# Spreading the sums of weights over two blocks, and a seventh weight buffer in block 4

## The chip, the core and the metric

The kernel runs on one core of a Trainium2 chip. The metric is the device time of one execution in microseconds (us), the median of several runs. The engines are TensorE (PE in the profile), VectorE (DVE), ScalarE (ACT), GpSimd (POOL) and SyncE (SP), which here does nothing but issue transfers.

## What is computed

Three stages follow one another, on 3072 tokens of width 512, all in float32.

```
for t in range(768):                       # 4 batches x 8 heads x 64
    state = gamma * state + k_t v_t^T
    y_t   = scale * q_t state              # decaying attention
x  = y                                     # 3072 tokens x 512
xn = x / sqrt(mean(x*x) + 1e-6) * rms_g
x  = (silu(xn @ w_gate) * (xn @ w_val)) @ w_out          # d_ff 1536
h  = x @ w_in                                            # d_ff 1024
s  = h * softmax(h)
out = ((s - mean s) / sqrt(var s + 1e-6) * g_ln) @ w_out2
```

## The kernel before

The tokens are worked in six blocks of 512, numbered 0 to 5. Attention of the next block runs inside the matmuls of the block in hand, as do the norm of the next block and the second feed-forward layer of the last one. A float32 operand is split into a high and a low half (tiles ending in h and l: `xnh`, `xnl`), and each product is three matmuls, hi x hi, lo x hi and hi x lo (L844 to L846).

In blocks 0 to 3 (`bc_block`) the inner width 1536 is cut into twelve pieces m of 128. Each m has three phases on TensorE: gate (bank GB, followed by the silu on ScalarE, L896), value (bank VB, followed by the product on VectorE, L865, whose result is split at L101 and L102), and out (bank X, with the tiles `wo`). Each phase ends at a slot, so a block has 36 slots of the first layer, a few us each, and some more for the second. Side work is hung on the slots as lists of Python functions (`extra`); tables at the head of the file say which slot. The order on each engine comes from a scheduler that keeps these lists roughly in order.

Blocks 4 and 5 (`shared_block` and `seven_block`, L960) use a seven-product scheme for pairs of m: instead of eight products of quarter blocks there are seven, of sums of quarters. For this the kernel prepares sums of the weights in blocks 1 to 3: `sums_steps(j, part, n)` adds two weight tiles on POOL (L622), then takes four quarter sums (L641), splits the results on VectorE and ScalarE (`parts`), and stores them to DRAM (`sscr`, L656 and L658). Two tiles take part, X (the sums) and H (the split results of its first half). `SUMS` and `LATE_SUMS` give the block and the slot. `w2_sums(k)` does the same for the second layer's weights (L674, L680, stored to `t2scr`), and `W2_SUMS_AT` gives its slots in block 2.

Four resources order this work. The tag `x2` has four rotating tiles of 512 KB, which the sums use in blocks 1 to 3; a new tile waits until the store of the tile's last user has landed. POOL is one queue in order: behind the sums stand the decay of the attention state (L282), which VectorE's update of the state (L279) waits for, and behind that update, on VectorE, the row sums of the norm (L350) and the product L865. SP is one queue too: a transfer that waits for a tile holds up all that stand behind it. DMA semaphores are eight, taken in turn.

In block 4 the weights and their sums come as half tiles, fourteen to a pair j of m, two to a 512 KB buffer (`fit`); six buffers rotate, four of tag `w4` and two of tag `x2`. L1056 and L1058 load a buffer in one transfer, L1061 in two. The first two `wo` tiles of block 4 are issued from slot 56 of block 3 (L773), ahead of the seventh buffer load, and their tiles are free once POOL has split the last tiles of x (L102).

Of the kernel before, what the change touches and what calls it, by code (L numbers as in the profile page):

```python
# [36 lines left out]
SUMS = {1: [(3, 0), (3, 1)], 2: [(0, 0), (0, 1), (1, 0), (1, 1), (4, 0)], 3: [(2, 0), (2, 1), (4, 1)]}  # L37
LATE_SUMS = {(3, 1): (5, 0), (3, 5): (5, 1)}
W2_SUMS_AT = (13, 20)
# [4 lines left out]
def retention_moe_kernel(ctx: ExitStack, tc: tile.TileContext, qk0, q2, kt, kv, wpk, w2i, w2o,  # L44
# [564 lines left out]
    def sums_steps(j, part, n):  # L609

        X, H = [], []
        small = n == 1 and part == 0

        def pair(t):
            if small:
                t.extend(wt("A" if t is X else "r2", [P, 512], F32, 2 if t is X else 8) for _ in range(2))
            else:
                x = wt("x2", [P, 2, 512], F32, 4)
                t.extend((x[:, 0, :], x[:, 1, :], x))

# [31 lines left out]
        def store():  # L652
            for t, at in ((H, 0), (X, 2)):
                if small:
                    for i in range(2):
                        nc.sync.dma_start(sscr[j][part][:, at + i], t[i].rearrange("p (s x) -> p s x", s=2))  # L656
                else:
                    nc.sync.dma_start(sscr[j][part][:, at:at + 2], t[2].rearrange("p a (s x) -> p a s x", s=2))  # L658

        if (j, part) in SUMS.get(n, ()):  # L660
            at0, at1 = 6 * j + part, 6 * j + 3 + part
            return {at0: [lambda: whole(0)], at1: [lambda: whole(1), sums], at1 + 2: [parts], at1 + 3: [store]}
        return {0: [load], 2: [both, sums], 4: [parts], 5: [store]}
# [3 lines left out]
    def w2_sums(k):  # L667
# [18 lines left out]
        def parts():  # L686
            for t in (W[0][:, 0, :], W[1][:, 1, :]):
                o.append(wt("x2", [P, 2, 512], F32R, 4))
                tied(o[-1][:, 0, :], o[-1][:, 1, :], t)

        def parts2():
            tied(w2["h"][:, k, 512:], w2["l"][:, k, 512:], W[1][:, 0, :])
            h, l = (wt("st", [P, 512], F32R, 3) for _ in range(2))
            tied(h, l, W[0][:, 1, :])
            o.extend((h, l))

        def store():
            for i in range(2):
                nc.sync.dma_start(t2scr[i][:, :, k, :], o[i].bitcast(F32))

        def store2():
            for i in range(2):
                nc.sync.dma_start(t2scr[2][:, i, k, :], o[2 + i].bitcast(F32))
# [338 lines left out]
    def fit_load(tiles):  # L1042

        def source(j, part, q):
            if q in (0, 4, 6):
                return scr[2 * j + (q == 6)][part][:, :, lo if q == 0 else hi]
            return sscr[j][part][:, (0, 2, 3, None, 1)[q - 1]]

        for T in tiles:
            t = fit[T % len(fit)]  # L1050
            tf = t.bitcast(F32)
            keys = [((2 * T + i) // 14, (2 * T + i) // 7 % 2, (2 * T + i) % 7) for i in range(2)]
            stock.update((key, t[:, i]) for i, key in enumerate(keys))
            (j, part, q), S = keys[0], sscr[keys[0][0]][keys[0][1]]
            if q == 2:
                nc.sync.dma_start(tf, S[:, 2:4])  # L1056
            elif q == 1:
                nc.sync.dma_start(tf.rearrange("p a s x -> p a (s x)"), S[:, 0:3:2].rearrange("p a s x -> p a (s x)"))  # L1058
            else:
                for i, key in enumerate(keys):  # L1060
                    nc.sync.dma_start(tf[:, i], source(*key))  # L1061

    NT = 7 * NM // 2

    def fit_first(n):
        fit.extend(wt("w4", [P, 2, 2, 256], F32R, 4) for _ in range(4))
        fit_load(range(2))
# [4 lines left out]
    def fit_last(n):  # L1072
        fit.extend(wt("x2", [P, 2, 2, 256], F32R, 4) for _ in range(2))
        fit_load(range(4, 6))

    def shared_block(n):
# [3 lines left out]
        pairs = [(wt("r2", [P, 512], F32R, 8), wt("r2", [P, 512], F32R, 8)) for _ in range(3)]  # L1080
# [30 lines left out]
        def last_outs():  # L1111
            t, w = fit[2].rearrange("p a b x -> p a (b x)"), tuple(wt("A", [P, 512], F32R, 2) for _ in range(2))
            nc.sync.dma_start(t.bitcast(F32), scr[NM - 2][2])
            for k in range(2):
                nc.sync.dma_start(w[k].bitcast(F32), scr[NM - 1][2][:, k, :])
            wsp[base + NM - 2, 2], wsp[base + NM - 1, 2] = t, w

        for j in range(NM // 2):
            m = 2 * j
            final = m == NM - 2  # L1120
            g = phase1(j, 0)
            slot(n, 6 * j)
# [18 lines left out]
            if final:  # L1141
                out(m - 2, range(3, NK))
# [7 lines left out]
            for i in range(2):  # L1150
                if i:
                    V.tensor_tensor(out=vf[:, 512:], in0=vf[:, 512:], in1=gf[:, 512:], op=ALU.mult)
                ah, al = pairs[nact[0] % 3]
# [4 lines left out]
            if final:  # L1158
                out(m - 1)
# [421 lines left out]
    for n in range(NB):  # L1581
        if n + 1 < NB:
# [15 lines left out]
            if n + 1 in SEVEN:  # L1598
                r = (30, 32) + ((33, 34, 34, 34, 34) if n + 1 < NB - 1 else (35,) * 5) + (36, 50, 50, 50)
                r += (39, 40, 41, 42) if n + 1 == NB - 1 else (54, 54, 54, 55)  # L1600
                begun7, more7 = (lambda: seven_load(n + 1), seven_pump) if n + 1 == NB - 1 else \
                    (lambda: fit_first(n + 1), lambda: fit_more(n + 1))
                first7 = [begun7] + [lambda i=i: w_load((n + 1) * NM + i, 2) for i in range(2)] + [more7]
                if n + 1 < NB - 1:
                    extra.setdefault((n, 54), []).append(lambda: fit_last(n + 1))
                for s, f in zip((47, 48, 48, 51) if n + 1 == NB - 1 else (47, 56, 56, 51), first7):
# [95 lines left out]
```

## Time and profile before

| | |
|---|---|
| median of three runs | 982.71 us (981.64 to 983.69) |
| profiled execution | 981.34 us, of which its span is 979.5 us |
| PE busy | 955.9 us, 98% of the span |
| DVE, ACT, POOL busy | 557.7, 418.0, 462.0 us |
| bytes moved | 230.91 MB, 236 GB/s in the mean |

TensorE is busy nearly throughout. What is left over is some 24 us of idle time in the span, at a few places, and the time that matmuls take longer where the granted clock is low. The page's mean rates hide how uneven the transfers are: in some stretches of block 4 the DMA engines are busy without a break, while just before they have little to do.

### The profile page before, as it was taken

Reading aid. Unit: us, or ns where it says so; the run is one execution under the profiler, and the core shown is the slowest. Engines: PE = TensorE matmul, PEld = TensorE weight load, DVE = VectorE, ACT = ScalarE, POOL = GpSimd, SP = SyncE. Lnnn points to the kernel's source line nnn. Section 1 sums busy time; section 2 is a strip of 40 time slices with the busy share of each in tenths; the row PEclk is TensorE's granted clock in tenths of the full one; section 3 lists DMA queues with packets and bytes.
Section 4 is the critical chain, followed back from the end, with each engine's and each line's share of the span. In section 5 each row is a group of like instructions: output and inputs, shape, how many; then the busy total and the mean of one; then the engine's idle time right before and its main releaser. Section 6 shows DMA issues by size and latency. Waiting matters only on the chain.

```text
span 979.5 us, 18179 instructions
## 1 busy us (share of the span) xinstructions
PE 955.9 (98%) x6852; PEld 805.3 (82%) x6852; DVE 557.7 (57%) x1126; ACT 418.0 (43%) x831; POOL 462.0 (47%) x497
## 2 busy tenths in 40 slices
PE   8999999999999999989999999999899999999998
PEld 7878787887887888778888888888788988999987
DVE  4788766565375644465574442574555467343473
ACT  3757656475344343223454231346212256321254
POOL 6876853696053394784538344546111166000022
PEclk9799999999999999999999999999999999999999
DMA  9699999897823306989824889823999936688501
GB/s 342 232 321 398 362 321 349 300 342 252 296 61 97 94 22 228 295 303 295 320 98 148 295 267 297 285 95 96 284 287 350 302 127 220 215 302 293 192 1 44
DMA packets 98887, 230.91 MB, mean 236 GB/s; under 512 B 11632, under 2 KB 38640, under 8 KB 97776
## 3 DMA queue, kind: packets, MB, share of 16 engines
q1 hardware_dynamic: 90016, 204.59, 62.6%
q10 hardware_dynamic: 8784, 25.17, 6.7%
q8 instruction: 54, 0.88, 0.4%
q14 instruction: 33, 0.27, 0.1%
HBM read 187.77 MB, written 41.94 MB: 235 GB/s over the span
## 4 chain that ended last, share of the span: by engine, by line
PE 77%; DMA 8%; DVE 5%; POOL 3%; ACT 3%; issue 1%; SPq 0%; ACTq 0%; POOLq 0%; DVEq 0%
PE X L844 9%; PE X L846 9%; PE X L845 9%; PE GB L844 5%; PE GB L845 5%; PE GB L846 5%; PE VB L960 4%; PE VB L844 4%; PE VB L845 4%; PE VB L846 4%; PE GB L960 3%; PE X L1359 3%; PE SB L122 3%; PE GB L1359 2%; PE VB L1359 2%; PE YB L960 2%
## 5 line engine op out<-in xcount | busy, mean ns | idle before, releaser
L845 PE MATMUL X<-r,wo 128*128 128x512 f32 x252 | 99.0, 393 | 0.0
L745 POOL TENSOR_TENSOR st<-st,x 128x512 int32<-128x512 int32 x52 | 70.3, 1353 | 59.6 <-ACT x L742 21.4
L846 PE MATMUL X<-r,wo 128*128 128x512 f32 x252 | 98.3, 391 | 0.0
L844 PE MATMUL X<-r,wo 128*128 128x512 f32 x252 | 96.4, 399 | 1.0 <-ACT r L101 1.0
L865 DVE TENSOR_TENSOR f<-VB,f 128x512 f32<-128x512 f32 x48 | 33.1, 689 | 69.2 <-PE VB L846 56.8
L101 ACT CAST r<-f 128x512 fp32r<-128x512 f32 x60 | 37.1, 620 | 80.5 <-DVE f L865 60.7
L844 PE MATMUL VB<-xnh,w 128*128 128x512 f32 (+1 forms) x172 | 68.0, 395 | 3.1 <-DVE f L865 3.1
L102 DVE TENSOR_TENSOR r<-f,r 128x512 fp32r<-128x512 f32 x60 | 58.1, 969 | 19.3 <-ACT r L101 18.6
L844 PE MATMUL GB<-xnh,w 128*128 128x512 f32 (+1 forms) x172 | 67.7, 393 | 0.9 <-ACT f L896 0.5
L845 PE MATMUL GB<-xnl,w 128*128 128x512 f32 (+1 forms) x172 | 67.1, 390 | 0.5 <-DVE xnl L102 0.4
L846 PE MATMUL VB<-xnh,w 128*128 128x512 f32 (+1 forms) x172 | 67.1, 390 | 0.3 <-POOL w L102 0.3
L845 PE MATMUL VB<-xnl,w 128*128 128x512 f32 (+1 forms) x172 | 67.1, 390 | 0.0
L846 PE MATMUL GB<-xnh,w 128*128 128x512 f32 (+1 forms) x172 | 66.7, 388 | 0.0
L282 POOL TENSOR_TENSOR U<-U,u 128x256 f32<-128x256 f32 x27 | 17.7, 654 | 96.6 <-PE YB L122 59.2
L102 POOL TENSOR_TENSOR r<-st,r 128x512 fp32r<-128x512 f32 x4 | 5.2, 1300 | 116.3 <-ACT r L101 116.3
L896 ACT ACTIVATE f<-GB 128x512 f32<-128x512 f32 x48 | 28.5, 594 | 69.8 <-PE GB L846 69.6
L844 PE MATMUL X<-w2oh,r 128*128 128x512 f32 (+1 forms) x144 | 56.6, 393 | 0.5 <-ACT r L1222 0.5
L844 PEld LDWEIGHTS X<-r,wo 128*128 128x128 f32 x252 | 47.5, 190 | 10.8 <-ACT r L101 1.1
L846 PE MATMUL X<-w2oh,r 128*128 128x512 f32 (+1 forms) x144 | 56.1, 390 | 0.2 <-DVE r L1223 0.2
L846 PEld LDWEIGHTS X<-r,wo 128*128 128x128 f32 x252 | 47.5, 188 | 10.0
L845 PE MATMUL X<-w2ol,r 128*128 128x512 f32 (+1 forms) x144 | 55.5, 385 | 0.0
L845 PEld LDWEIGHTS X<-r,wo 128*128 128x128 f32 x252 | 47.6, 189 | 9.5 <-issue 0.2
(511 smaller groups left out, 2751.0 us busy)
## 6 DMA issues: line engine op xcount, KB each, us to landing
w<-scr SPq DMA_DIRECT2D x73, 512.0 KB, 6.0
wo<-scr SPq DMA_DIRECT2D x57, 512.0 KB, 5.5
x<-in_wpk SPq DMA_DIRECT2D x36, 512.0 KB, 6.6
sscr<-x SPq DMA_DIRECT2D x22, 512.0 KB, 6.0
rv<-in_kv SPq DMA_DIRECT2D x40, 256.0 KB, 6.5
scr<-CV ACTq DMA_DIRECT2D x18, 512.0 KB, 6.7
w<-scr SPq DMA_DIRECT2D x34, 256.0 KB, 5.8
w<-sscr SPq DMA_DIRECT2D x14, 512.0 KB, 5.9
```

What stands on the lines that cost most here:

```text
L101: h = nc.scalar.copy(hi, src)
L102: (lo_eng or nc.vector).tensor_tensor(out=lo, in0=src, in1=hi.bitcast(F32), op=ALU.subtract)
L122: return lambda: nc.tensor.matmul(out, lhsT=lhsT, rhs=rhs, start=start, stop=stop)
L282: nc.gpsimd.tensor_tensor(out=new, in0=old, in1=u64.unsqueeze(2).to_broadcast([P, 4, 64]), op=ALU.mult)
L745: nc.gpsimd.tensor_tensor(out=ti, in0=ti, in1=lo, op=ALU.add)
L844: nc.tensor.matmul(ps, lhsT=lh, rhs=rh, start=start, stop=False)
L845: nc.tensor.matmul(ps, lhsT=lh, rhs=rl, start=False, stop=False)
L846: return nc.tensor.matmul(ps, lhsT=ll, rhs=rh, start=False, stop=stop)
L865: recent["dve"] = nc.vector.tensor_tensor(out=a, in0=GV[1], in1=silu[:, 0, :], op=ALU.mult)
L896: recent["act"] = nc.scalar.activation(s[:, 0, :], GV[0], AF.Silu)
L960: recent["seven"] = nc.tensor.matmul(ps, lhsT=x, rhs=y[:, k, :], start=start and k + i == 0, stop=k == 1 and i == 2, skip_group_check=True)
L1359: last["mm"] = nc.tensor.matmul(bank, lhsT=x[:, k, ts_], rhs=y[:, k, :], start=start and k + i == 0, stop=k == 1 and i == 2, skip_group_ch ...
```

## The change

Five sums stay where they were or change their block: in block 2 the sums of (0,0), (1,0) and (4,0) remain, and (0,1) and (1,1) move to block 3. Splits come one or two slots later than before, stores two slots after the split. The late sum (5,0) is loaded one slot later, (5,1) nineteen slots later. The second layer's sums start one slot and two slots earlier (12 and 18 for 13 and 20); their splits no longer take `x2` tiles of their own but are written in place, and their stores are cut accordingly. In block 3 the H tiles of (0,1) and (1,1) are pairs of tag `r2`.

In block 4 a seventh weight buffer is made of two tiles of tag `r2`; for that the pairs that hold the split product go from three to two. The first two `wo` tiles are issued behind the loads of the buffers. Two of the four steps that sum quarters of x move from slot 54 to 53 of block 3. The last out(m - 1) of block 4 is called earlier.

```diff
-SUMS = {1: [(3, 0), (3, 1)], 2: [(0, 0), (0, 1), (1, 0), (1, 1), (4, 0)], 3: [(2, 0), (2, 1), (4, 1)]}
-LATE_SUMS = {(3, 1): (5, 0), (3, 5): (5, 1)}
-W2_SUMS_AT = (13, 20)
+SUMS = {1: [(3, 0), (3, 1)], 2: [(0, 0), (1, 0), (4, 0)], 3: [(0, 1), (1, 1), (2, 0), (2, 1), (4, 1)]}
+LATE_SUMS = {(3, 2): (5, 0), (3, 24): (5, 1)}
+W2_SUMS_AT = (12, 18)
...
-        small = n == 1 and part == 0
+        tags = {(1, 0): ("A", "r2"), (3, 1): ("x2", "r2")}.get((n, part) if n == 1 or j < 2 else None, ("x2", "x2"))
...
-            return {at0: [lambda: whole(0)], at1: [lambda: whole(1), sums], at1 + 2: [parts], at1 + 3: [store]}
-        return {0: [load], 2: [both, sums], 4: [parts], 5: [store]}
+            wait = 2 if j == 4 else 4 if (j, 1 - part) in SUMS[n] and part else 3
+            return {at0: [lambda: whole(0)], at1: [lambda: whole(1), sums], at1 + wait: [parts],
+                    at1 + wait + 2: [store]}
+        return {0: [load], 2: [both, sums], 4: [parts], 6: [store]}
...
         def parts():
-            for t in (W[0][:, 0, :], W[1][:, 1, :]):
-                o.append(wt("x2", [P, 2, 512], F32R, 4))
-                tied(o[-1][:, 0, :], o[-1][:, 1, :], t)
+            tied(w2["h"][:, k, 512:], w2["l"][:, k, 512:], W[1][:, 0, :])
+            tied(W[1][:, 0, :].bitcast(F32R), W[1][:, 1, :].bitcast(F32R), W[1][:, 1, :])
...
+    def fit_room(tag, n):
+        for _ in range(n):
+            if tag == "r2":
+                fit.append((None, [wt("r2", [P, 2, 256], F32R, 8) for _ in range(2)]))
+            else:
+                t = wt(tag, [P, 2, 2, 256], F32R, 4)
+                fit.append((t, [t[:, 0], t[:, 1]]))
...
+    def fit_outs(n):
+        for i in range(2):
+            with tc.issue_after(recent["fit"].ins):
+                w_load(n * NM + i, 2)
...
-        pairs = [(wt("r2", [P, 512], F32R, 8), wt("r2", [P, 512], F32R, 8)) for _ in range(3)]
+        pairs = [(wt("r2", [P, 512], F32R, 8), wt("r2", [P, 512], F32R, 8)) for _ in range(2)]
+        fit_room("r2", 1)
+        fit_load([len(fit) - 1])
...
             g = phase1(j, 0)
+            if j == 0:
+                fit_outs(n)
...
-                r += (39, 40, 41, 42) if n + 1 == NB - 1 else (54, 54, 54, 55)
+                r += (39, 40, 41, 42) if n + 1 == NB - 1 else (53, 53, 54, 55)
```

Three places show how the order moves. The first is POOL in block 2, where the second layer's sums begin. In the rows `x_478` and `x_479` (before) and `x_471` and `x_472` (now) are the `x2` tiles of the first of these sums, `x_451` and `x_456` tiles of first-layer sums, `U` the attention state; at the end of a row stand the engines and DMA semaphores that it waits for. Before:

```order
L641 TENSOR_TENSOR x_456_3878<-x_456_3878 128x256 [waits Pool_49]
L674 TENSOR_TENSOR x_478_4107<-w2ih,w2il 128x1024 [waits DMAHW5_49,DMAHW2_49,DVE_49]
L282 TENSOR_TENSOR U_80<-U_81,u_146 128x256 [waits PE_49]
L674 TENSOR_TENSOR x_479_4109<-w2ih,w2il 128x1024 [waits DMAHW7_49,DVE_49]
L680 TENSOR_TENSOR x_478_4107<-x_478_4107 128x512 [waits Pool_49]
L282 TENSOR_TENSOR U_81<-U_80,u_146 128x256 [waits DVE_49,Pool_49]
```

Now:

```order
L677 TENSOR_TENSOR x_471_4046<-w2ih,w2il 128x1024
L642 TENSOR_TENSOR x_451_3840<-x_451_3840 128x256 [waits Pool_49]
L683 TENSOR_TENSOR x_471_4046<-x_471_4046 128x512 [waits Pool_49]
L677 TENSOR_TENSOR x_472_4048<-w2ih,w2il 128x1024 [waits DMAHW1_49,DVE_49]
L642 TENSOR_TENSOR x_451_3840<-x_451_3840 128x256 [waits Pool_49]
L683 TENSOR_TENSOR x_471_4046<-x_472_4048,x_471_4046 128x512 [waits Pool_49]
L642 TENSOR_TENSOR x_451_3840<-x_451_3840 128x256 [waits Pool_49]
L683 TENSOR_TENSOR x_472_4048<-x_472_4048,x_471_4046 128x512 [waits Pool_49]
L642 TENSOR_TENSOR x_451_3840<-x_451_3840 128x256 [waits Pool_49]
L683 TENSOR_TENSOR x_472_4048<-x_472_4048 128x512 [waits Pool_49]
L282 TENSOR_TENSOR U_80<-U_81,u_146 128x256 [waits DVE_49,PE_49]
```

The first L674 waited for two stores and stood ahead of the decay L282; its counterpart, L677, waits for none, the second L677 for one, and all of the first sum's work now stands ahead of the decay.

The second place is SP at the start of block 4: `w`, `x` and `r` are the buffers of weights and sums, `wo` the tiles of out, `rk` and `rq` attention's. Before:

```order
L773 DMA wo_6666<-scr_2_89 128x1024
L1061 DMA w_740_6403<-scr_1_91 128x2x256
L1061 DMA w_741_6404<-scr_0_93 128x2x256
L1061 DMA w_741_6404<-sscr_0_125 128x512
L773 DMA wo_6668<-scr_2_92 128x1024
L222 DMA rk_6870<-in_kt 64x2x256
L223 DMA rq_6869<-in_q 64x2x256
L222 DMA rk_6870<-in_kt 64x2x256
L223 DMA rq_6869<-in_q 64x2x256
L1056 DMA w_742_6405<-sscr_0_125 128x1024
```

Now:

```order
L1061 DMA x_766_6630<-sscr_1_124 128x2x512
L1061 DMA w_738_6405<-scr_0_93 128x2x256
L1061 DMA x_767_6631<-sscr_1_124 128x512
L1061 DMA x_767_6631<-scr_1_88 128x2x256
L1061 DMA r_776_6687<-sscr_1_124 128x512
L1061 DMA r_777_6688<-scr_1_91 128x2x256
L1061 DMA w_738_6405<-sscr_0_125 128x512
L1061 DMA w_739_6406<-sscr_0_125 128x1024
L774 DMA wo_6724<-scr_2_89 128x1024
L774 DMA wo_6726<-scr_2_92 128x1024
```

The two `wo` loads stood ahead of the half tile `w_741<-scr_0_93` and of the buffer loaded from `sscr_0_125`; now they stand behind that buffer, and two half loads into `r` tiles are new.

The third is SP in the second half of block 3. The loads `x_679` and `x_680` belong to the late sum (5,1), which stood far ahead of this place before; `w_679` and `w_675` are the gate weights of m = 9. Before:

```order
L773 DMA w_673_5853<-scr_0_111 128x1024 [waits DMAHW0_49,PE_49]
L658 DMA sscr_1_128<-x_663_5753 128x1024 [waits DMAHW1_49,DVE_49]
L773 DMA w_676_5871<-scr_1_112 128x1024 [waits DMAHW2_49,PE_49]
L658 DMA sscr_1_128<-x_649_5614 128x1024 [waits DMAHW3_49,DVE_49]
L773 DMA wo_5869<-scr_2_110 128x1024 [waits DMAHW4_49,PE_49]
L228 DMA qd_5844<-in_q 64x512 [waits DMAHW5_49,PE_49]
L228 DMA qd_5844<-in_q 64x512 [waits DMAHW6_49]
L226 DMA rv_5843<-in_kv 64x2x512 [waits DMAHW7_49,PE_49]
L226 DMA rv_5843<-in_kv 64x2x512 [waits DMAHW0_49]
L773 DMA w_679_5902<-scr_0_114 128x1024 [waits DMAHW1_49,PE_49]
L773 DMA w_684_5955<-scr_1_115 128x1024 [waits DMAHW2_49,PE_49]
```

Now:

```order
L659 DMA sscr_0_127<-x_658_5724 128x1024 [waits DMAHW7_49,DVE_49]
L774 DMA w_672_5851<-scr_1_112 128x1024 [waits DMAHW0_49,PE_49]
L659 DMA sscr_1_128<-x_668_5824 128x1024 [waits DMAHW1_49,DVE_49,Activation_49]
L659 DMA sscr_0_127<-x_640_5565 128x1024 [waits DMAHW2_49,DVE_49]
L633 DMA x_679_5935<-scr_1_118 128x1024 [waits DMAHW7_49,DMAHW3_49]
L774 DMA wo_5849<-scr_2_110 128x1024 [waits DMAHW4_49,PE_49]
L228 DMA qd_5813<-in_q 64x512 [waits DMAHW5_49,PE_49]
L228 DMA qd_5813<-in_q 64x512 [waits DMAHW6_49]
L659 DMA sscr_1_128<-x_645_5593 128x1024 [waits DVE_49]
L633 DMA x_680_5937<-scr_1_121 128x1024 [waits DMAHW1_49,DMAHW0_49]
L226 DMA rv_5812<-in_kv 64x2x512 [waits PE_49]
L226 DMA rv_5812<-in_kv 64x2x512 [waits DMAHW2_49]
L774 DMA w_675_5884<-scr_0_114 128x1024 [waits DMAHW3_49,PE_49]
```

Each of the two loads waits for a DMA semaphore beside its own turn (two names of DMAHW), that is, for a store of an earlier sum to have landed, and the tiles `rv` and the weights of m = 9 stand behind both.

## Rows read from the trace of the kernel before

**Rows 1.** Waits of PE over the span: line, awaited line, us in total, times, longest.

```profile
PE VB L960 <- DMA w<-sscr: 2.6, 1, 2.6
...
PE GB L844 <- ACT f L896: 0.5, 1, 0.5
```

**Rows 2.** Timeline of PE, block 2: start, us, line, tiles, idle before and its releaser.

```profile
418.81 0.50 PE L844 MATMUL VB<-xnh,w 128*128 128x512 f32 x1 [3.07 <-DVE f L865]
```

**Rows 3.** Timeline of DVE, block 2, from the state's update to the product.

```profile
414.78 0.28 DVE L279 TENSOR_TENSOR U<-U,SB 64x128 f32<-64x128 f32 x1 [5.41 <-POOL U L282]
415.07 0.59 DVE L279 TENSOR_TENSOR U<-U,YB 64x128 f32<-64x128 f32 x2
...
416.99 1.04 DVE L350 TENSOR_REDUCE ssq<-sq 128x128 f32<-128x512 f32 x1 [1.01 <-ACT sq L347]
418.06 0.69 DVE L865 TENSOR_TENSOR f<-VB,f 128x512 f32<-128x512 f32 x1
```

**Rows 4.** ACT's copies of the state's output (L344), whole span: idle before them, by releaser.

```profile
DVE U L279: 33.1, 12
PE GB L846: 6.8, 1
```

**Rows 5.** Timeline of POOL, block 2.

```profile
398.77 5.80 POOL L641 TENSOR_TENSOR x<-x 128x256 f32<-128x256 f32 x8
411.78 2.39 POOL L674 TENSOR_TENSOR x<-w2ih,w2il 128x1024 f32<-128x1024 f32 x1 [7.21 <-DMA sscr<-x]
414.13 0.61 POOL L282 TENSOR_TENSOR U<-U,u 128x256 f32<-128x256 f32 x1
...
419.82 1.72 POOL L680 TENSOR_TENSOR x<-x,x 128x512 f32<-128x512 f32 x1
```

**Rows 6.** Windows: stretch, its length, busy by engine, granted clock, DMA share, GB/s.

```profile
420.00:425.00 5.00, 5.00 (x61) 3.67 (x60) 2.27 (x3) 0.41 (x1) 5.00 (x4) 0.66 0.66 252
...
668.00:684.00 16.00, 15.82 (x87) 13.17 (x85) 5.64 (x14) 10.10 (x18) 11.63 (x19) 1.00 0.21 67
...
690.00:740.00 50.00, 45.38 (x532) 41.21 (x531) 27.54 (x64) 10.13 (x23) 8.86 (x10) 1.00 1.03 295
```

**Rows 7.** Timeline of SP, block 2: the weights of m = 4, and a store.

```profile
394.64 2.02 SPq L773 DMA_DIRECT2D w<-scr  x2
...
404.87 0.32 SPq L658 DMA_DIRECT2D sscr<-x  x1
```

**Rows 8.** Timeline of PE, block 4: the three waits, and out(4) behind the third.

```profile
697.97 0.95 PE L960 MATMUL VB<-x,w 128*128 128x256 f32 x6 [2.61 <-DMA w<-sscr]
...
707.28 0.97 PE L960 MATMUL GB<-x,x 128*128 128x256 f32 x6 [0.99 <-DMA x<-sscr]
...
735.43 0.95 PE L960 MATMUL VB<-x,x 128*128 128x256 f32 x6 [0.82 <-DMA x<-sscr]
...
736.94 0.86 PE L844 MATMUL X<-r,wo 128*128 128x512 f32 x3
```

**Rows 9.** Timeline of SP, block 4.

```profile
682.02 0.33 SPq L773 DMA_DIRECT2D wo<-scr  x1
...
687.90 0.55 SPq L1056 DMA_DIRECT2D w<-sscr  x1
...
725.88 0.51 SPq L773 DMA_DIRECT2D wo<-scr  x1
726.93 0.33 SPq L1056 DMA_DIRECT2D x<-sscr  x1
```

**Rows 10.** Timelines of SP and PE, block 3: a store, w(9), GB(9) and VB(9).

```profile
584.62 0.32 SPq L658 DMA_DIRECT2D sscr<-x  x1
...
592.38 3.05 SPq L773 DMA_DIRECT2D w<-scr  x2
...
606.88 0.39 PE L844 MATMUL GB<-xnh,w 128*128 128x512 f32 x1
...
609.60 0.39 PE L844 MATMUL VB<-xnh,w 128*128 128x512 f32 x1
```

More of the change, by code (lines that the diff above doesn't have):

```diff
@@ L611, in sums_steps @@
         X, H = [], []
-        small = n == 1 and part == 0
+        tags = {(1, 0): ("A", "r2"), (3, 1): ("x2", "r2")}.get((n, part) if n == 1 or j < 2 else None, ("x2", "x2"))
         def pair(t):
-            if small:
-                t.extend(wt("A" if t is X else "r2", [P, 512], F32, 2 if t is X else 8) for _ in range(2))
-            else:
+            tag = tags[t is H]
+            if tag == "x2":
                 x = wt("x2", [P, 2, 512], F32, 4)
                 t.extend((x[:, 0, :], x[:, 1, :], x))
+            else:
+                t.extend(wt(tag, [P, 512], F32, {"A": 2, "r2": 8}[tag]) for _ in range(2))
         def add(i, w):
@@ L653, in store @@
             for t, at in ((H, 0), (X, 2)):
-                if small:
+                if len(t) == 2:
                     for i in range(2):
@@ L1049, in fit_load @@
         for T in tiles:
-            t = fit[T % len(fit)]
-            tf = t.bitcast(F32)
+            t, halves_ = fit[T % len(fit)]
             keys = [((2 * T + i) // 14, (2 * T + i) // 7 % 2, (2 * T + i) % 7) for i in range(2)]
-            stock.update((key, t[:, i]) for i, key in enumerate(keys))
+            stock.update(zip(keys, halves_))
             (j, part, q), S = keys[0], sscr[keys[0][0]][keys[0][1]]
[L1055 to L1058, printed above, removed]
-            else:
-                for i, key in enumerate(keys):
-                    nc.sync.dma_start(tf[:, i], source(*key))
+            both = {1: S[:, 0:3:2], 2: S[:, 2:4]}.get(q) if t is not None else None
+            if both is not None:
+                pairs = [(t.rearrange("p a s x -> p a (s x)"), both.rearrange("p a s x -> p a (s x)"))]
+            else:
+                pairs = [(h, source(*key)) for h, key in zip(halves_, keys)]
+            for to, src in pairs:
+                recent["fit"] = nc.sync.dma_start(to.bitcast(F32), src)
+    def fit_room(tag, n):
+        for _ in range(n):
+            if tag == "r2":
+                fit.append((None, [wt("r2", [P, 2, 256], F32R, 8) for _ in range(2)]))
+            else:
+                t = wt(tag, [P, 2, 2, 256], F32R, 4)
+                fit.append((t, [t[:, 0], t[:, 1]]))
     NT = 7 * NM // 2
+    LAST = 38
     def fit_first(n):
-        fit.extend(wt("w4", [P, 2, 2, 256], F32R, 4) for _ in range(4))
+        fit_room("w4", 4)
         fit_load(range(2))
@@ L1072, in fit_last @@
     def fit_last(n):
-        fit.extend(wt("x2", [P, 2, 2, 256], F32R, 4) for _ in range(2))
+        fit_room("x2", 2)
         fit_load(range(4, 6))
+    def fit_outs(n):
+        for i in range(2):
+            with tc.issue_after(recent["fit"].ins):
+                w_load(n * NM + i, 2)
     def shared_block(n):
@@ L1111, in last_outs @@
         def last_outs():
-            t, w = fit[2].rearrange("p a b x -> p a (b x)"), tuple(wt("A", [P, 512], F32R, 2) for _ in range(2))
+            t, w = fit[LAST % len(fit)][0].rearrange("p a b x -> p a (b x)"), tuple(wt("A", [P, 512], F32R, 2) for _ in range(2))
             nc.sync.dma_start(t.bitcast(F32), scr[NM - 2][2])
@@ L1141, in shared_block @@
             if final:
-                out(m - 2, range(3, NK))
+                out(m - 2, range(3, NK)), out(m - 1)
             v = v[0]
@@ L1157, in shared_block @@
                 acts[m + i] = (ah, al)
-            if final:
-                out(m - 1)
             slot(n, 6 * j + 5)
```

22 lines of the change are left out of this document (11 added, 11 removed).

## The prediction

> **What bounds the kernel now.** I read the totals of busy time first: PE is busy for 98% of the span, so whatever the change does to the other engines counts only where a matmul waits, or where matmuls run at a lower clock. Then the list of PE's waits [rows 1] and its timeline [rows 2, 8]. The change touches four of these places: one wait of 3.07 us in block 2 [rows 2], three in block 4 of 2.61, 0.99 and 0.82 us [rows 8], and a small one of 0.5 us in block 1 [rows 1]. Last the windows, for the clock and the transfers [rows 6]. The reader is to see there that the stretch right behind the wait of block 2 has a granted clock of 0.66 (a mean of the levels 1.2 and 2.4 GHz), while the 50 us around the 2.61 us wait of block 4 have 1.00. So the long wait costs its own 3.07 us and then 5.00 x (1 - 0.66) = 1.7 us of slower matmuls; those of block 4 cost themselves alone.
>
> **Block 2: why PE waits.** Backwards from the matmul: it waits for the product L865, which ends at 418.75; L350 stands ahead of that on VectorE and waits for ScalarE's squares; ScalarE's copies of the state's output wait for the update L279, which started at 414.78 after standing 5.41 us for the decay L282 [rows 3]. The profile names another releaser for these copies, a matmul of GB (6.8 us); I take the twelve others, which are all put down to L279, and the end of the second update, 415.07 + 0.59 = 415.66, as showing the true one [rows 3, 4]. L282 (414.13) is ready before that but queued on POOL behind L674, which stood 7.21 us for a store to land so that its `x2` tile came free [rows 5].
>
> **What the change does there.** Two of the four first-layer sums leave, and the second layer's sums need no `x2` tiles for their splits, so the first L677 waits for no store. The second waits for one, the first store of the sum (0,0), which stands on SP between the two weight loads that were issued from 394.64 on [rows 7]: issued about 395.2. A store took 411.78 - 404.87 = 6.9 us to land [rows 5, 7], so it lands near 402.1. From the second L677 (2.39) to L282 there now stand three quarter sums of 5.80 / 8 = 0.73 and three L683, which I price like an L680, at 1.72 each or less [rows 5]: 2.39 + 2.2 + 5.2 = 9.8 us. L282 then starts near 411.9, against 414.13. The way from L282 to the end of L865 was 418.75 - 414.13 = 4.6 us [rows 3, 5], so L865 ends near 416.5. PE could have begun at 418.81 - 3.07 = 415.74. What stays is 0.8 us, or less where an L683 is shorter; if the store goes out behind the second weight load, at 396.7, it is 2.3. I take 0.5. The wait shrinks by 2.6 and the slow stretch of 1.7 goes with it: -4.3. Bounds: 0, if the decay is as late as before, and -4.8.
>
> The second of these sums now stands ahead of the next decay in the same manner, two slots earlier than before, while PE is some 4 us earlier too. It had no wait before; I take 0, with the first one's 3.07 as the upper bound [rows 2].
>
> **Block 1.** The silu that GB waits for stood 0.5 us behind a load [rows 1]. Stores of the sum (3,1) now come a slot or two later, which clears SP for that load. I take -0.3, between 0 and -0.5.
>
> **Block 4.** Up to 682.02 SP stood at the first `wo` load, and the transfers were nearly idle (share 0.21); after that they are the limit (share 1.03, 295 GB/s) [rows 6, 9]. The tile that ends the first wait was issued at 687.90 and released PE at 697.97, ten us later [rows 8, 9], so what counts is the bytes ahead of it. Before: two `wo` of 0.5 MB, three half tiles of 0.25, attention's tiles 0.5, and its own 0.5, together 2.75 MB. Now: three half tiles (two in the new `r` buffer) and itself, 1.25 MB. The 1.5 MB at 295 GB/s are 5.1 us, more than 2.61: the first wait goes. The second needs its tile 2.61 + 0.99 = 3.6 us earlier. 4.25 MB are ahead instead of 5.0, which gives 2.5, and the seventh buffer lets SP issue some 0.4 earlier: 0.7 remain. The third needs 2.61 + 0.99 + 0.82 = 4.4 us; its tile has 12.1 MB ahead instead of 13.4, which gives 4.4. It comes just in time.
>
> But the bytes are moved, not removed. The 1.3 MB that the third tile overtakes are attention's tiles and the `wo` of out(4), which had been issued just ahead of it at 725.88 [rows 9] and now comes behind it. The whole set is the 13.4 MB that had landed when PE went on at 735.43. So out(4), which started at 736.94 without a wait [rows 8], cannot start before about 735.0. With the other waits gone PE would be there at 736.94 - 4.4 = 732.5 and meets a new wait of about 2.4 us there. The gain of block 4 is therefore some 2.0 us, to which I add 0.2 because SP no longer stands at 682: -2.2, with bounds of 0 and -4.6. That the pairs of split products go from three to two I cost at nothing: twelve matmuls of out lie between two uses of a pair, 2.7 us as of GB(9) [rows 10], and hide one copy and one subtraction. If that cover were gone it would be within the same bounds.
>
> Here the Trainium skill would have it otherwise. Its page "DMA: Bandwidth & Descriptors", section "Anatomy of one DMA — SWDGE (gpsimd) path", gives a transfer (there one issued from GpSimd) a fixed cost of about 2.0 us and its bytes at 436 GB/s; for 0.5 MB that is an estimate of 3.2 us. The row disagrees in this stretch, with ten us. By that rule out(4)'s tile would be there in time, which is the fourth rival below.
>
> **Block 3.** Two sums are added, and (5,1) is loaded at slot 24. SP now meets its two loads, each of which waits for a store to have landed, ahead of the weights of m = 9. Before, these were issued at 592.38 and needed at 606.88, 14.5 us later; at the 8.5 us that the tile of 726.93 took to 735.43 [rows 8, 9] the lead is 6.0 us, at ten it is 4.5. Now: a store goes out near 584.6, as one did before [rows 10], and lands 6.9 later, at 591.5; the store that the second load awaits comes one slot later (a phase of 2.7 us [rows 10]), near 588 to 590.5, and lands at 595 to 597.4; then two `rv` loads, and the weights at 597 to 600, 4.6 to 7.6 us later than before. Against the lead that is a wait of 0 to 3.1 us, to which a slow stretch of 1.7 may come: 0 to +4.8, and I take +0.6. POOL's sum of (5,1) waits for the same loads; the decay behind it is needed some 5 us later than it was done, and I take nothing for it. At the block's start two additions on POOL stand ahead of a split of x: +0.3 for that and all that I haven't seen, between 0 and +2.
>
> **The sum.** -4.3 - 0.3 - 2.2 + 0.6 + 0.3 = -5.9 us, against the profiled execution's own 981.34 (span 979.5 and 1.84 around it): 975.4. The median of the runs shown is 982.71, 1.37 above that execution, and it is medians that are compared: **976.8 us**. Less than 0.2% (2 us) from 982.7 can hardly be told from no change here.
>
> **The rivals.** First: block 4 gains nothing, because the queue of bytes is what it is and PE's waits only change their tile. For it: share 1.03 [rows 6]. Against it: SP stood until 682.02 with idle DMA engines ahead. 976.8 + 2.2 = 979.0.
>
> Second: block 2's wait only changes its cause. POOL's chain ahead of L282 has grown from one L674 to two and four L683; if the store lands some 2.3 us later than I put it, the decay is where it was, wait and slow stretch with it. 976.8 + 4.3 = 981.1.
>
> Third, the other side: SP's two loads in block 3. If a store takes ten us to land, as the tile in block 4 did, both waits stand one behind the other, 2 x 10 = 20 us from 584.6 on; the weights of m = 9 go out at about 607 and land at 615, 8.5 us after GB(9) wants them, and the clock falls with it for 1.7. 976.8 - 0.6 + 10.2 = 986.4. It decides from a wait of about 6.5 us on (less is hidden by what the other blocks gain). Against it: both stores are issued before the first landing, so the waits overlap.
>
> Fourth: transfers in block 4 behave by bare issue, out(4) does not wait, and block 4 gives its whole 4.4 us: 976.8 - 2.2 = 974.6.
>
> **How the numbers follow.** My forecast 0.52, with a range of its own from 974 to 979.5; first rival 0.14, second 0.13, third 0.13, fourth 0.08. Faster by over 0.2% (under 980.7) are the forecast but for 0.02 of it, the first and fourth but for 0.01, and a third of the second: 0.76, of which I give 0.04 to what I have overlooked: 0.72. Slower by over 0.2% (over 984.7): 0.11 of the third and 0.04 overlooked, 0.15. Same: the rest, 0.13. For 8 in 10 the range leaves out 0.05 below, the fourth with all other terms at their good ends (973.2), and the third above; it ends at 983.0, behind the second rival with its later chain.
>
> **What would show it.** Right: no wait of PE at L844 for L865 near 416, a clock of 1.00 behind it, and L677 there without 7 us of idle; in block 4 no wait at the first tile from `sscr` and a new one, about 2 us, at X with `wo` near 735 of the old time; SP at the two loads of block 3 for some us, and the weights of m = 9 landing within 2 us of GB(9). Wrong: a wait of PE for the weights of m = 9 over 4 us, an L282 that starts after 414, or waits for `sscr` tiles in block 4 as long as before.

## The result and the profile after

The changed kernel took 972.94 us in the median of four runs (971.94 to 974.81), the kernel before 982.17 (979.04 to 983.69); the ratio of the two is 0.9912, with an interval of 0.9883 to 0.9942. The forecast was 976.8 against 982.71, a ratio of 0.994: faster, as forecast, but by about 9 us and not 5.9. As a bare number the median lies just under 973.2, the lower end of the range for 8 in 10; the ratio times the earlier median, 974.1, lies inside it. A second series of the same kernel (below) gave 0.9919.

PE's waits in the profile after, longest first (line, awaited line, total us, times, longest; line numbers from 620 on are one to sixteen higher than before):

```profile
PE X L845 <- ACT r L101: 2.8, 2, 1.8
PE YB L122 <- DMA KV<-in_kv: 1.6, 1, 1.6
...
PE X L845 <- DMA wo<-scr: 0.4, 1, 0.4
...
PE VB L961 <- DVE f L1119: 0.3, 1, 0.3
```

The waits of [rows 1, 2, 8] for L865 and for `sscr` tiles in block 4 are gone from the list, and so is the one for the silu of block 1. Two of those that are new matter here: X waits 1.84 us for L101 in block 3, and X waits 0.36 us for a `wo` tile, which is out(4). The windows of the profile after, behind block 2's old place and behind the new wait (length, busy by engine, granted clock, DMA share, GB/s):

```profile
412.84:417.84 5.00, 5.00 (x67) 3.97 (x66) 3.35 (x4) 3.28 (x6) 1.94 (x1) 1.00 0.98 319
628.50:633.50 5.00, 5.00 (x15) 3.95 (x16) 1.94 (x4) 1.85 (x5) 4.22 (x3) 0.66 0.88 362
```

Against [rows 6] the slow stretch has moved from block 2 to block 3 (0.66 both times).

PE issues 6852 matmuls in both kernels, in the same order but for 88 places in a few short stretches, so the start of each can be compared with its start before; the difference is PE's lead, and a time with the lead added to it is a time in the old frame. In the two profiled executions (981.34 and 974.81 us, 6.5 apart) the lead grows and shrinks like this: 2.2 us ahead of block 1's silu, nearly all in the first 34 us, which the change does not touch (the wait for `KV` was 3.0 us there and is 1.6, and matmuls beside it ran slowly for less long); 0.6 in block 1; 4.9 at block 2's old wait, of which 0.5 is lost again by the block's end; then 4.1 us are lost in block 3, 0.4 at GB(9) and 3.7 at the new wait; 4.1 gained in block 4; 0.5 lost to the end. The start varies from execution to execution by more (the lead there lies between -3.9 and 2.2 us in the profiles of this document); it is no part of the change.

The lead matters for the rates too. By the clock, the two windows of block 4 [rows 6] now read 188 and 320 GB/s and not 67 and 295, but PE is 3 to 7 us further on in them, so they are not the same work. Cut by the same matmuls, the 16 us ahead of block 4's tiles carry 165 GB/s and not 67, and the stretch from there to out(4) carries 295 and not 289 (the first line is from before, the others from after):

```profile
684.00:736.94 52.94, 48.32 (x607) 44.49 (x606) 30.34 (x73) 11.62 (x26) 9.35 (x11) 1.00 1.02 289
```

```profile
664.80:680.80 16.00, 15.82 (x89) 13.38 (x87) 5.86 (x14) 9.93 (x19) 12.35 (x19) 1.00 0.53 165
680.80:729.74 48.94, 48.03 (x606) 44.39 (x605) 29.60 (x74) 11.74 (x27) 7.91 (x10) 1.00 1.04 295
```

### The profile page after: what moved, and what is told of

It is laid out like the page before. It is cut to its first block, busy times and chain, and to the rows that moved or that the text cites. A ratio compares the mean times of both kernels' runs of the same rounds, so it can differ in the third digit from the quotient of the medians.

```text
span 972.9 us, 18176 instructions
## 1 busy us (share of the span) xinstructions
PE 952.5 (98%) x6852; PEld 802.0 (82%) x6852; DVE 566.3 (58%) x1126; ACT 417.5 (43%) x831; POOL 465.6 (48%) x497
## 4 chain that ended last, share of the span: by engine, by line
PE 75%; DMA 8%; DVE 5%; POOL 4%; ACT 3%; issue 2%; SPq 1%; ACTq 0%; POOLq 0%; DVEq 0%
PE X L845 9%; PE X L847 9%; PE X L846 9%; PE GB L845 5%; PE GB L847 5%; PE GB L846 5%; PE VB L961 4%; PE VB L845 4%; PE VB L846 4%; PE VB L847 4%; PE GB L961 3%; PE X L1375 3%; DMA rv<-in_kv 3%; PE SB L122 3%; PE GB L1375 2%; PE VB L1375 2%
## 5 line engine op out<-in xcount | busy, mean ns | idle before, releaser
L101 ACT CAST r<-f 128x512 fp32r<-128x512 f32 x60 | 37.1, 620 | 92.5 <-DVE f L866 72.6
L866 DVE TENSOR_TENSOR f<-VB,f 128x512 f32<-128x512 f32 x48 | 33.0, 688 | 62.2 <-PE VB L847 46.8
L102 DVE TENSOR_TENSOR r<-f,r 128x512 fp32r<-128x512 f32 x60 | 57.8, 964 | 18.9 <-ACT r L101 18.2
L282 POOL TENSOR_TENSOR U<-U,u 128x256 f32<-128x256 f32 x27 | 17.7, 654 | 103.8 <-PE YB L122 50.0
L102 POOL TENSOR_TENSOR r<-st,r 128x512 fp32r<-128x512 f32 x4 | 5.2, 1296 | 111.0 <-ACT r L101 111.0
```

The source lines that it names most:

```text
L101: h = nc.scalar.copy(hi, src)
L102: (lo_eng or nc.vector).tensor_tensor(out=lo, in0=src, in1=hi.bitcast(F32), op=ALU.subtract)
L282: nc.gpsimd.tensor_tensor(out=new, in0=old, in1=u64.unsqueeze(2).to_broadcast([P, 4, 64]), op=ALU.mult)
L866: recent["dve"] = nc.vector.tensor_tensor(out=a, in0=GV[1], in1=silu[:, 0, :], op=ALU.mult)
```

## The experiments

Each ran beside the kernel before on the same chip; ratios are to it. Lines of the edits that only follow from the ones shown are left out.

**Each half alone.** The first has block 4 as before:

```diff
-        pairs = [(wt("r2", [P, 512], F32R, 8), wt("r2", [P, 512], F32R, 8)) for _ in range(2)]
-        fit_room("r2", 1)
-        fit_load([len(fit) - 1])
+        pairs = [(wt("r2", [P, 512], F32R, 8), wt("r2", [P, 512], F32R, 8)) for _ in range(3)]
...
-            if j == 0:
-                fit_outs(n)
+                    first7 += [(56, lambda i=i: w_load((n + 1) * NM + i, 2)) for i in range(2)]
-                r += (39, 40, 41, 42) if n + 1 == NB - 1 else (53, 53, 54, 55)
+                r += (39, 40, 41, 42) if n + 1 == NB - 1 else (54, 54, 54, 55)
```

> The changed kernel with block 4 as before (six buffers, three pairs, wo from slot 56, x sums at slots 54 and 55). Theory: the parts add up. Block 2's wait of 3.07 us and the slow stretch behind it are gone (-4.5 us against before), the three waits of block 4 (2.61, 0.99, 0.82) are back, and block 3 has the new wait for the product of m = 11, some 1.8 us with 1.6 us of slow matmuls, because that comes from the sums and not from block 4. Sum: 2 to 4 us faster than before, so a ratio of 0.996 to 0.998. Rival: the wait in block 3 comes from transfers for the seventh buffer or from the moved steps of x; then it is absent here and the kernel is 5 us faster than before (0.995).

It took 0.9954 (0.9931 to 0.9977). Block 2's wait is gone, the three of block 4 are back, and block 3 has none. PE's waits from 400 to 745 us:

```profile
PE VB L961 <- DMA w<-sscr: 1.9, 1, 1.9
PE VB L961 <- DMA x<-sscr: 1.8, 1, 1.8
PE GB L961 <- DMA x<-sscr: 1.4, 1, 1.4
```

The second has the sums' code and tables as before and block 4 as changed:

```diff
-SUMS = {1: [(3, 0), (3, 1)], 2: [(0, 0), (1, 0), (4, 0)], 3: [(0, 1), (1, 1), (2, 0), (2, 1), (4, 1)]}
-LATE_SUMS = {(3, 2): (5, 0), (3, 24): (5, 1)}
-W2_SUMS_AT = (12, 18)
+SUMS = {1: [(3, 0), (3, 1)], 2: [(0, 0), (0, 1), (1, 0), (1, 1), (4, 0)], 3: [(2, 0), (2, 1), (4, 1)]}
+LATE_SUMS = {(3, 1): (5, 0), (3, 5): (5, 1)}
+W2_SUMS_AT = (13, 20)
```

> The kernel before with block 4's part alone (seventh buffer, two pairs, wo behind the buffers, x sums at 53). Theory: block 2's wait of 3.07 us with its slow stretch stays, block 4 gains 4 us (no wait over 0.5 us between 690 and 740), block 3 has no new wait: a ratio of 0.996. Rival: block 4's gain needs what the sums free; then its waits stay above 2 us in all and the ratio is 0.998 to 1.0.

It took 0.9979 (0.9953 to 1.0005). Its waits over the same stretch, and two windows, the first from block 4's start to out(4):

```profile
PE VB L844 <- DVE f L865: 4.9, 1, 4.9
PE X L844 <- DMA wo<-scr: 3.2, 1, 3.2
PE VB L960 <- DMA w<-sscr: 0.6, 1, 0.6
```

```profile
686.75:739.51 52.76, 48.45 (x606) 44.49 (x605) 30.28 (x75) 11.74 (x27) 7.90 (x10) 1.00 1.02 277
739.50:744.50 5.00, 4.99 (x18) 4.13 (x19) 0.00 (x0) 0.00 (x0) 0.77 (x1) 0.68 1.05 378
```

Here the new wait that the prediction put at out(4), 2.4 us, does come: 3.2 us, with a slow stretch behind it, in a profile whose transfers ran at 277 GB/s up to there. In the changed kernel, at 295, it is 0.36. So it is real, and it goes with the transfers' rate; why the rate was lower here is not shown. The profile is also the slowest of this kernel's twelve runs (985.54 us, with a median of 978.07), so its waits need not be the usual ones. The ratio says that the two halves do not simply add up to 0.9912, though the intervals allow it (0.0046 + 0.0021 against 0.0088).

**The wait in block 3.** In the profile after, the chain reads backwards from PE through DVE and POOL to SP:

```profile
628.50 1.30 PE L845 MATMUL X<-r,wo 128*128 128x512 f32 x4 [1.84 <-ACT r L101]
```

```profile
626.44 0.71 DVE L426 STREAM_TRANSPOSE ssq<-rsum 128x512 f32<-128x512 f32 x1 [7.86 <-POOL rsum L422]
627.07 0.65 DVE L866 TENSOR_TENSOR f<-VB,f 128x512 f32<-128x512 f32 x1
```

```profile
621.23 1.04 POOL L245 TENSOR_TENSOR kd<-rv,ktab_t 128x512 f32<-128x512 f32 x1 [8.73 <-PE GB L847]
622.23 1.29 POOL L250 TENSOR_TENSOR qd<-qd,qtab_t 128x512 f32<-128x512 f32 x1
623.48 2.92 POOL L422 TENSOR_TENSOR rsum<-rsum,mhalf 128x16 f32<-128x16 f32 x1
```

The reader should distrust one name: L245 reads the tile `rv`, whose second load was issued at 611.73 and landed at 621.08; the GB matmul is put down only because it ended last. Behind L245 and L250 on POOL stands the norm's power L422, behind that on VectorE the transpose L426, and behind that the product L866 for the last out of the block. Three kernels ask whether that is so, and whether it is a fixed cost. In the first, the products of k and q with their decay tables come later on POOL:

```diff
-                if nxt:
+                if nxt and nxt == NCB * 5:
+                    extra.setdefault((3, 37), []).append(lambda: att_prep(nxt))
+                elif nxt:
                     att_prep(nxt)
```

> The changed kernel, but the products of k and q with their decay tables for the chunk after the block (L245, L250, which wait for the rv tile) are issued behind the norm's steps on POOL in block 3. Theory: the wait of PE for the last product of block 3 comes from POOL standing for rv (landing at 621.1) ahead of the norm's power L422, which VectorE's transpose L426 waits for, with L866 queued behind it. Then the wait of 1.84 us and the slow stretch of 1.6 us go, and the kernel is 3.5 us faster than the changed one in its profile, 0.987 to 0.990 of before. Rival: the product is late for another reason (the transfers themselves); then the wait stays at 1.5 us or more and the time is that of the changed kernel (0.991).

The wait is gone, but the time is no better than the changed kernel's: 0.9939 (0.9918 to 0.996), above 0.9912, with intervals that overlap. PE's waits from 600 to 685 us, and POOL where the two pairs of products went:

```profile
PE X L849 <- DVE r L1241: 0.8, 1, 0.8
PE X L1237 <- DVE f L1225: 0.6, 1, 0.6
PE GB L849 <- DVE r L1241: 0.3, 1, 0.3
```

```profile
644.20 1.04 POOL L245 TENSOR_TENSOR kd<-rv,ktab_t 128x512 f32<-128x512 f32 x1
...
647.91 1.45 POOL L250 TENSOR_TENSOR qd<-qd,qtab_t 128x512 f32<-128x512 f32 x1
649.33 0.37 POOL L1248 TENSOR_TENSOR sm<-sm 128x1 f32<-128x1 f32 x1
```

Both pairs moved, not one, since they keep their order, and 5 us of work now stand ahead of the softmax's small steps (L1248) in the second layer, which PE then waits for: its lead falls by 2.2 us between 650 and 678 of the old frame, and again by 2.3 in the later kernel with the same edit. The expectation had the cause right (the profiles below bear it out) and the cost of the cure wrong. The second kernel moves the late sum's traffic out of block 3:

```diff
-LATE_SUMS = {(3, 2): (5, 0), (3, 24): (5, 1)}
+LATE_SUMS = {(3, 2): (5, 0), (2, 28): (5, 1)}
```

> The changed kernel with the late sum (5,1) loaded at slot 28 of block 2 instead of slot 24 of block 3. Theory: rv lands late in block 3 because the two loads and two stores of (5,1), 2 MB, lie ahead of it while the DMA engines are busy throughout (share 1.05); without them rv lands some 5 us earlier and the wait for the last product goes, -3.5 us against the changed kernel, unless block 2 pays for it. Rival: PE has only caught up with transfers that were never earlier; then rv lands at about 621 as before and the wait stays.

No wait in block 3, and 0.9913 (0.9883 to 0.9943), the changed kernel's time and not 3.5 us less. The third is the changed kernel, profiled again:

> The changed kernel unaltered, a second profile. Theory: the wait of 1.84 us for the last product of block 3 and the slow matmuls behind it belong to one execution in which the rv tile landed at 621.1 in saturated transfers; here the wait is under 0.6 us, and the median over the runs lies at 0.991 of before. Rival: it is a fixed cost of the changed order, 1.5 us or more again, which kd_late takes away; then kd_late's ratio is 0.003 below this one.

It took 0.9919 (0.9896 to 0.9942), and the same place has

```profile
PE X L845 <- ACT r L101: 0.4, 1, 0.4
```

```profile
628.00:633.00 5.00, 4.59 (x20) 3.49 (x20) 2.42 (x5) 1.37 (x3) 4.17 (x4) 1.00 0.97 373
```

0.41 us and no slow stretch. So the 3.7 us of the first profile are not a fixed cost. Seven profiles of this document have (5,1) loaded at slot 24 of block 3 and the products in their old place on POOL. In these, POOL stood 8.7, 8.2, 6.9, 6.6, 6.5, 5.7 and 5.5 us for `rv`; PE waited 1.84 us behind the first, 0.41 behind the second, and not at all behind the other five. In all seven L422 starts right behind L250, so `rv` sets its time. In the five profiles in which (5,1) is loaded earlier and the products stand as before, POOL stood 3.9 to 5.2 us, and L422 then waited 0.7 to 1.4 us more for an operand of its own, so `rv` sets nothing there. POOL in one of each kind, with early `wo` (below) and with (5,1) in block 2:

```profile
617.71 1.59 POOL L245 TENSOR_TENSOR kd<-rv,ktab_t 128x512 f32<-128x512 f32 x1 [5.46 <-DMA rv<-in_kv]
619.27 1.29 POOL L250 TENSOR_TENSOR qd<-qd,qtab_t 128x512 f32<-128x512 f32 x1
620.52 2.92 POOL L422 TENSOR_TENSOR rsum<-rsum,mhalf 128x16 f32<-128x16 f32 x1
```

```profile
620.54 1.47 POOL L250 TENSOR_TENSOR qd<-qd,qtab_t 128x512 f32<-128x512 f32 x1
622.72 2.92 POOL L422 TENSOR_TENSOR rsum<-rsum,mhalf 128x16 f32<-128x16 f32 x1 [0.71 <-DVE rsum L421]
```

So the loads of (5,1) at slot 24 do put `rv` on the path, but it becomes a wait of PE only in the executions in which POOL stands longest for it, two of seven here. That is why taking the traffic away gains nothing in the median. Whether their bytes or their place on SP ahead of `rv` does it was not separated.

**Block 4: the buffer or the order.** The change did three things there: the buffer (with one pair less), the order, and the two steps of x at slot 53. No kernel takes back the steps of x alone. One takes back the order of the `wo` loads and keeps the seventh buffer:

```diff
-            if j == 0:
-                fit_outs(n)
...
+                    first7 += [(56, lambda i=i: w_load((n + 1) * NM + i, 2)) for i in range(2)]
```

> The changed kernel with the first two wo loads of block 4 issued from slot 56 of block 3, as before. Theory: what the first wait hung on is the bytes ahead of the tile and SP's stand for POOL; with two wo loads (1 MB, 3.4 us at 295 GB/s) ahead of buffers again and SP standing for them, the first tile from sscr lands late and PE waits 1.5 to 3 us there, while out(4) does not wait. 1.5 to 3 us slower than the changed kernel. Rival: the seventh buffer did it alone, then no wait comes back over 0.6 us and the time is that of the changed kernel.

The other keeps the order and takes back the buffer:

```diff
-        pairs = [(wt("r2", [P, 512], F32R, 8), wt("r2", [P, 512], F32R, 8)) for _ in range(2)]
-        fit_room("r2", 1)
-        fit_load([len(fit) - 1])
+        pairs = [(wt("r2", [P, 512], F32R, 8), wt("r2", [P, 512], F32R, 8)) for _ in range(3)]
```

> The changed kernel with six buffers and three pairs, the wo loads still behind the buffers. Theory: the first wait stays away since the wo loads are behind, but half a megabyte less is ahead of PE at every tile, so the second and third waits come back with 1 us each: 1 to 2.5 us slower than the changed kernel. Rival: the seventh buffer does nothing and no wait comes back.

With seven buffers and `wo` early: 0.9889 (0.987 to 0.9909). With six and `wo` late: 0.9952 (0.9932 to 0.9973). PE's waits from 400 to 745 us, and the 16 us ahead of block 4's tiles (the same matmuls as above), first for the one, then for the other:

```profile
PE VB L961 <- DVE f L1119: 0.3, 1, 0.3
...
```

```profile
662.10:678.10 16.00, 15.81 (x91) 13.28 (x93) 5.68 (x14) 10.09 (x18) 12.19 (x19) 1.00 0.63 206
```

```profile
PE GB L961 <- DMA x<-sscr: 1.2, 1, 1.2
PE VB L961 <- DMA x<-sscr: 1.0, 1, 1.0
PE VB L961 <- DVE f L1117: 0.3, 1, 0.3
```

```profile
662.30:678.30 16.00, 15.82 (x91) 13.23 (x93) 5.64 (x14) 10.07 (x18) 12.13 (x19) 1.00 0.45 149
```

The first wait is gone in both: with the sums alone it is 1.9 us, with `wo` late or with the buffer none. But both also keep the moved steps of x, and an early `wo` load waits for just the splits (L102) that these bring forward on POOL, from 679.3 to 673.6 in the old frame. The waits of SP for them, before and in the kernel with early `wo`:

```profile
SPq L773 <- POOL x L102: 12.1, 1, 12.1
```

```profile
SPq L774 <- POOL x L102: 4.1, 1, 4.1
```

So the first `wo` load goes out 5.5 us earlier in the old frame though its place is the old one, and whether the moved steps alone remove the first wait was not tried. The second and third wait go only with the buffer. From 650 to 745 of the old frame PE's lead shrinks by 0.9 us in the kernel with the sums alone; it grows by 2.0 with six buffers, by 4.1 in the changed kernel and by 4.7 with seven buffers and early `wo`. By these single profiles, and counted from the kernel with the sums alone, the order with the moved steps is worth 2.9 us and the buffer 2.1 more. With the buffer the order of `wo` buys nothing; early, its 1 MB moves in the stretch that has room (206 GB/s against 165), and out(4) does not wait. The expectation (1.5 to 3 us slower) was wrong.

**Block 2: which half of the sums.** Two kernels divide that part. The changed kernel with the second layer's sums as before:

```diff
-W2_SUMS_AT = (12, 18)
+W2_SUMS_AT = (13, 20)
...
-            tied(w2["h"][:, k, 512:], w2["l"][:, k, 512:], W[1][:, 0, :])
-            tied(W[1][:, 0, :].bitcast(F32R), W[1][:, 1, :].bitcast(F32R), W[1][:, 1, :])
+            for t in (W[0][:, 0, :], W[1][:, 1, :]):
+                o.append(wt("x2", [P, 2, 512], F32R, 4))
+                tied(o[-1][:, 0, :], o[-1][:, 1, :], t)
```

> The changed kernel with the second layer's sums as before: slots 13 and 20, splits in two x2 tiles of their own. Theory: block 2's wait hung on the first L674 standing for a store of a first-layer sum, and with two of these sums gone the store it needs is out some 10 us earlier; so the wait at VB stays under 1 us and the time is within 1 us of the changed kernel. Rival: the two more tiles per sum are what made it wait; then L677 stands 4 us or more and PE waits over 1.5 us at VB or at the next product, with a slow stretch.

0.9926 (0.9897 to 0.9954), and no wait in block 2. The kernel before with only the second layer's sums changed, the same diff the other way round:

> The kernel before with the second layer's sums alone as in the change (slots 12 and 18, split in place). Theory, after the run in which these sums stood as before and no wait came back: block 2's wait hangs on the five first-layer sums in block 2, so it stays here; the first L674 stands for a store that no slot change brings forward, and since the decay is now behind both L674 the wait is 4 us or more with a slow stretch: 0 to 3 us slower than before. Rival: either half is enough to remove it; then no wait at VB and 4 us faster than before (0.996).

1.0041 (1.0019 to 1.0063), slower than before. Its largest wait of PE, and POOL ahead of it:

```profile
PE VB L842 <- DVE f L863: 8.5, 1, 8.5
```

```profile
408.95 1.62 POOL L680 TENSOR_TENSOR x<-x 128x512 f32<-128x512 f32 x1
415.22 2.37 POOL L674 TENSOR_TENSOR x<-w2ih,w2il 128x1024 f32<-128x1024 f32 x1 [4.64 <-DMA sscr<-x]
417.66 1.26 POOL L680 TENSOR_TENSOR x<-x,x 128x512 f32<-128x512 f32 x1
418.88 0.79 POOL L282 TENSOR_TENSOR U<-U,u 128x256 f32<-128x256 f32 x1
```

Here the second L674 stands for the store, and the decay L282 behind it starts at 418.88, where it started at 414.13 [rows 5] (PE is 0.9 us behind its old time). What took block 2's wait away is the first-layer part of the change. Two sums leave the block there, and the splits and stores of the others come later; that it is the leaving and not the later slots is likely, but was not tried apart. The second layer's new form alone makes the wait worse. Its profile is the slowest of ten runs (993.52 us, with a median of 988.39), so 8.5 us may be more than the usual wait.

**A version that beats both.** Three more kernels, with edits shown above: early `wo` with the late products, early `wo` with (5,1) in block 2, and early `wo` once more.

> The changed kernel with the wo loads from slot 56 as before and with the decay products of k and q behind the norm's steps on POOL. Theory: both keep what they showed alone; no wait over 0.5 us in block 4 and no wait for the last product of block 3 in any execution: 0.988 to 0.989 of before, 2 to 3 us below the changed kernel. Rival: the order of wo is indifferent and the lower time of the run with early wo loads was the start of that series; then 0.991.

> The changed kernel with the wo loads from slot 56 and the sum (5,1) in block 2. Theory: as the kernel with early wo loads, 0.989, since block 3's wait is small in most executions; with less to move in block 3 the rv tile lands before 616. Rival: block 2 pays for the two loads there: a wait for weights or for a product in block 2 of over 1 us.

> The changed kernel with the wo loads from slot 56 once more, to see whether its lower time holds. Theory: the seventh buffer alone does block 4's work and wo loads behind the buffers only delay them, so again no wait in block 4 over 0.5 us and 0.989 of before. Rival: 0.991 to 0.992, the changed kernel's time.

They took 0.9931 (0.9908 to 0.9954), 0.9913 (0.9887 to 0.994) and 0.9891 (0.9865 to 0.9916). The late products cost 0.4% here, against early `wo` alone, and 0.2 to 0.3% above. Early `wo` alone held its value: 0.9889 and 0.9891 in two series, against 0.9912 and 0.9919 of the changed kernel. The intervals overlap, and with (5,1) moved the order of `wo` made no difference (0.9913 both times). In block 4 itself PE's lead grows by 4.7 us in three profiles with early `wo`, and by 3.8 to 4.4 in four with the changed order, so at most 0.9 us of the difference arises there. I call early `wo` the best version measured, not one that is shown to be better.

## Why the prediction was right, and where it was not

**Block 2: right, -4.4 for -4.3.** The first L677 stood for nothing, the decay was done early enough, and the slow stretch left with the wait. POOL after, to compare with [rows 5]:

```profile
397.32 2.40 POOL L677 TENSOR_TENSOR x<-w2ih,w2il 128x1024 f32<-128x1024 f32 x1
...
406.14 0.79 POOL L282 TENSOR_TENSOR U<-U,u 128x256 f32<-128x256 f32 x1
```

PE stood 2.7 us ahead of its old time there, so 406.14 is 408.9 in the old frame; I had 411.9. The second L677 did not stand either: I let it wait for a store that lands near 402, and it began at 397.3. The half microsecond that I left for it was 0 in this profile and 0.7 in that of the second kernel with early `wo`. Of the two reasons I gave, sums that leave and splits that need no tiles, only the first was needed. The second rival (the wait stays, its cause changes) is what the second layer's sums do when they are changed alone.

**Block 1: right in size, -0.6 for -0.3, the cause open.** The silu's wait of 0.55 is gone in all eleven profiles with the changed block 1. But of two more with block 1 as before, it is gone in one (block 4's part alone) and 0.94 us in the other (the second layer's sums alone). So it varies by itself, and that the later stores remove it is likely, not shown.

**Block 4: right in kind, -4.1 for -2.2.** The three waits went. The step that failed is the one that held the bytes fixed: "the whole set is the 13.4 MB that had landed when PE went on at 735.43", so out(4) "cannot start before about 735.0". It started at 729.74, which is 732.9 in the old frame (PE was 3.2 us ahead as it entered block 4). SP and PE in the profile after:

```profile
672.78 0.33 SPq L1061 DMA_DIRECT2D r<-sscr  x1
...
720.16 0.50 SPq L774 DMA_DIRECT2D wo<-scr  x1
```

```profile
729.74 0.47 PE L845 MATMUL X<-r,wo 128*128 128x512 f32 x1 [0.36 <-DMA wo<-scr]
```

I let the transfers begin at 682, as before, run at 295 GB/s, and gave 0.2 us for SP no longer standing there. They began earlier: SP's first loads to `r` tiles went out at 672.8, which is 676.0 in the old frame, and over the same 16 us of PE's work the transfers carried 165 - 67 = 98 GB/s more, 1.6 MB or some 5 us at 295. Part of that went into 1.3 MB more that had moved by then (17.1 MB from 668 of the old frame to out(4), against 15.8 up to 735.43 before), and 2.1 us reached out(4). The rate was as I had it, 295. Where it was 277, the predicted wait came (3.2 us). The fourth rival, the whole 4.4 us, is nearest, though not by its reason: the tile of out(4) took 9.6 us from its issue at 720.2 until PE went on. The fit of the Trainium skill ("DMA: Bandwidth & Descriptors", "Anatomy of one DMA — SWDGE (gpsimd) path"), by which 0.5 MB take 3.2 us as an estimate, for a transfer issued from GpSimd, does not describe this stretch after the change either. And of the gain that I put down to the order, 2.1 of 5.0 us belong to the buffer, and an unknown part to the moved steps of x, to which I gave no price.

**Block 3: the right suspects, the wrong place.** I priced the wait at GB(9): 0 to 3.1 us. It was 0.18. The weights of m = 9 were issued at 589.6 in the new time, 596.7 in the old frame, and landed at 600.0, ten us later, almost as the bound had it. (The awaited store I put near 588 to 590.5; one slot of 2.7 us behind 584.6 is 587.3, by which the weights come at 596, and they did.) The cost arose behind it, where I wrote that for POOL "I take nothing": not the sum of (5,1) but the next `rv`, landing 9 to 10 us after issue, held POOL, the norm's power and the last product. In the profiled run that was 3.7 us, within the bound of 4.8; in the second profile 0.7, near the 0.6 that I took, but by luck, since I had priced another wait; and in five profiles it was nothing. The third rival asked for both stores' waits to follow one another; they overlapped, as its counter-argument said.

**The sum.** -0.6 - 4.4 - 4.1 + 0.5 is -8.6 us with nothing lost in block 3, as in five profiles of seven, and -7.9 with block 3 as in the second profile; the ratio says 0.0088 of 982, 8.6. I had -5.9. The difference is block 4's 1.9 us, block 3's 0.6 and small terms.

## What to carry to other kernels

When loads are limited by bytes, find the moment from which they may flow before counting what stands ahead of a tile: here they started six microseconds earlier, in a stretch that had room, and the forecast had put 0.2 us on that. Compare rates over the same work and not over the same times: between 690 and 740 us the rate rose from 295 to 320 GB/s, over the same matmuls only from 289 to 295. When side work is taken off an in-order queue, ask of each part alone whether it clears the queue; in block 2 one half of the change was worth 4.4 us and the other half, by itself, cost 4. And a wait seen in one profile of a saturated stretch wants a second profile before it is cured: the cure here cost 2.2 us in both of its profiles, and the wait nothing in most.

## What the hardware showed unexpectedly

A short wait can cost the clock where a longer one does not. Behind the 1.84 us wait of the profile after, the granted clock was 0.66 for 5 us; behind the 2.61 us wait before the change [rows 8] it was 1.00, and behind three waits of 1.9, 1.4 and 1.8 us with the sums alone no matmul ran slowly. Behind 8.5 us it was 0.50, which is the lower level, 1.2 GHz, throughout:

```profile
425.00:430.00 5.00, 4.87 (x12) 3.80 (x12) 3.05 (x3) 3.28 (x6) 5.00 (x4) 0.50 1.04 330
```

So the length of a wait alone does not say whether the slow stretch follows. What else decides was not tried.
